# A planned order of 478 jobs replaced by another: gate and output weights at other places among the loads, weight sums among other key jobs

## The chip, the cores and the metric

The kernel runs on one core of a Trainium2 chip. A core has five engines with a queue of instructions each, which work side by side and wait for each other by semaphores: TensorE (PE: matmuls, with their weight loads listed as PEld), VectorE (DVE), ScalarE (ACT), GpSimd (POOL) and SyncE (SP), which here issues nearly all DMA transfers. Matmuls write to PSUM, eight banks; everything else lies in SBUF. The metric is the device time of one launch in microseconds (us), as a median of runs.

## The reference, cut to what matters

One transformer block on x of 2048 rows and 576 columns: modulated layer norm, linear attention over 32 heads of 18 columns with a softmax feature map, a gated residual, a second modulated layer norm, a feed-forward of width 4608 and a second gated residual.

```python
mod = (silu(c) @ w_mod).reshape(1, 6, 1, -1)
sa, ca, ga, sb, cb, gb = ...
h = layernorm(x) * (1 + ca) + sa
q, k, v = h @ wqkv                       # 32 heads of 18
phi_q = concat(softmax(q @ w_phi), softmax(-(q @ w_phi)))
phi_k = concat(softmax(k @ w_phi), softmax(-(k @ w_phi)))
kv, z = phi_k^T v, sum(phi_k)
x = x + ga * ((phi_q @ kv / (phi_q @ z + 1e-6)) @ wo)
h = layernorm(x) * (1 + cb) + sb
x = x + gb * (relu(h @ w1) @ w2)
```

## The kernel before, in words

The 2048 rows are 16 tiles of 128. Keys and values of all 16 tiles have to be summed up (kv) before the first tile can be attended, so the kernel has a long first part that is not a loop: it loads, folds the head matrices into the key and query weights, makes the six modulation rows, projects K, V and Q of all tiles, attends tiles 0 to 3 (4 and 5 begun), and runs the first two-tile block of the feed-forward. Then come seven blocks b = 1 to 7 of two tiles each: the output projection `project` (L967) of the next two tiles, the first layer `l1_seven` (L756), the second layer `l2`. The feed-forward multiplies 2 x 2 blocks of matrices with seven products instead of eight, which is why sums of blocks of the weights w1 and w2 have to be made beforehand on DVE.

The order of the first part is written out as one string, `ORDER`, of 478 words. A word is a job, with a tile or part number, and behind a colon the pair of PSUM banks that its result takes. A loop (L1141) calls the jobs one after the other; each puts its instructions at the end of the queues of its engines, and no scheduler moves them later. So a word's place sets its place in the queue of each engine it uses, and no instruction passes one ahead of it on the same engine.

```python
for word in ORDER.split():
    name, _, s = word.partition(":")
    ...
    if s:
        at[f, n] = pair(int(s))
    JOBS[f](*(() if n is None else (n,)))
```

The jobs that matter below, by engine:

- SP, loads: `Lx` and `Lt` (x by rows and transposed, blocks of tiles), `LwkT`, `LwqT`, `Lwv` (key, query and value weights), `Lwsc`, `Lwsh` (first modulation), `Lwsb`, `Lwcb` (second modulation), `Lwga`, `Lwgb` (gates), `Lwo` (output weight); `wl0` to `wl4` (parts of w1, L612), `w2a0` to `w2a2` and `w2b0`, `w2b1` (parts of w2), `wm0` to `wm7` (further copies of blocks of w1 as operands of the sums, L491; `wm0` and `wm1` take the room of tiles of x that `bn12` to `bn15` have read). `VRd` and `QRd` move the four correction rows of the value and query weights into place; `gaw`/`gar` and `gbw`/`gbr` pass the gate rows through memory; `sq`/`qi` store and load again the query features of tiles 4 to 15; `qt`, `ou`, `hT` are transposes by DMA (L363, L416).
- PE: `Z` (matmuls on zeros that fill idle time, L244), `FK` and `FQ` (folding), `sc`, `sh` (first modulation), `m2` (second modulation, 50 matmuls that read wsb and then wcb, L265), `ga`, `gb` (gate rows, L376), `KR`, `VR`, `QR` (correction rows, also L376), `T` (transposed statistics, L638), `K`, `V`, `Q` (projections of a tile, ten matmuls each, L282; `Ka`, `Kb` are two pieces of the first two), `kv` (L334), `nu` (attention of a tile, L404), `ot` and `ht` (transposes on PE), `W` or `wf`/`wr` (output projection; L957 and L964), `lm0` to `lm8` (first layer of block 0, L739), `pa0` to `pa13` (its second layer, L922).
- DVE: `bn` (statistics of a tile, L249 and L250), `sd` (silu of c), `sK` (sums of a tile's key features, L292), `qs` (the same for queries, L292 and L353), `vE` (scaling a tile of values out of PSUM, L316), `nO` (normalising the attention, L411 and L412), `xr`, `xR` (residual), `lb` (second statistics), `ap`, `hd`, `lu`, `lv`, `px`, `py`, `pf` (block 0), `tf` (sums of features for block 1, L851), `wt0` to `wt7` (sums of blocks of w1, L489), `td`, `tb`, `tc`, `te` (sums of parts of w2, three each, L515).
- ACT: `eK`, `eQ` (exponentials of a tile, L287), `FQra` (folded query weights out of PSUM), `xa` (scaling x by the modulation), `rK`, `sa`, `Tc`, `m2c`, `ha`, `aP`, `hS` and others. POOL: `pA`, `pR`, `pM` (key features), `xp`, `sp`, `qp`, `wo` (output weight times the gate row).

A bank pair is taken again only after the job that empties it: K by `eK`, V by `vE`, Q by `eQ`, FQ by `FQra`, and so on.

Of the kernel before, what the change touches and what calls it, by code (L numbers as in the profile page):

```python
# [42 lines left out]


ORDER = """
Lbdw LwkT Lx0 Lcc sx Lwsc Lwsh Lx2 Lid Lt0 Lwv Lx4 Lt1 Z11 Z1 FK Z2 fra2 frd1 sd rp fra4 LwqT bn1 bn0 frd3 Z3 sc ca
frr bn2 sh shc sa0 sp0 xu0 fra0 T0:0 xv0 Tc0 KR:3 bn3 mk KRh Ka0:1 KRd2 Lx6 sa2 sp2 KRd0 KRd1 VR:0 VRh KRd3 Kb0 eKa0
VRe Ka1:2 VRd bn5 Kb1 eKa1 sK0 Lwsb sK1 Lt2 FQ3:1 FQra3 T2:0 bn7 xp2 Tc2 FQ0:3 FQra0 rK0 K2:2 FQ4:0 K3:1 pR0 FQra4 pA0
bn9 V1:0 FQ2:3 bn6 eK2 pM1 Lwga V0:2 Lwcb eK3 FQra2 vE1 Lx10 V3:1 xp6 sK2 FQ1:3 xa4 FQra1 V2:0 vE0 sK3 rK2 ga:2 gac
gaw pA2 bn4 QR:3 QRh Lt4 vE3 QRe QRd sa4 vE2 m2:2 sp4 bn8 T4:3 Tc4 m2c K4:1 eK4 pM0 kv0 Lt3 wl0 bn10 bn14 pR2 K5:0 eK5  # L50
K6:2 bn11 sa8 kv1 eK6 sK4 pM2 kv2 xp14 K7:0 eK7 Lwgb sK5 Q0:1 pM3 w2b0 bn12 rK4 pA4 V5:2 eQ0 sK7 kv3 vE5 sp8 V4:0 vE4
T8:2 pR4 pM4 xa8 wm0 Tc8 xp10 pM5 Q1:1 K8:0 K9:2 eQ1 eK8 kv4 qs0 qp0 sK6 bn13 gb:1 Q2:0 Lwo eK9 wm3 kv5 rK6 pA6 gbc
Q3:2 V6:1 sK8 eQ2 pR6 eQ3 pM7 sK9 rK8 qs1 qp1 V7:0 pM6 pA8 bn15 sa12 sp12 pR8 pM8 vE7 vE6 V9:2 V8:0 vE9 kv6 K11:1
T12:2 xa12 vE8 wl1 pM9 K10:0 eK11 qs3 wm1 kv7 kv8 qs2 Lmask qp2 sK11 Tc12 qp3 w2a2 K12:1 eK10 sK10 eK12 Q5:2 rK10 pA10
eQ5 sK12 V11:0 vE11 kv9 K13:1 eK13 V10:0 vE10 gar sK13 K14:2 eK14 rK12 wo4 qt0 wt0 pR10 pM10 kv10 K15:0 pM11 kv11 wl3
eK15 pA12 sK14 Q4:2 eQ4 pR12 qt3 pM13 pM12 qt1 sK15 V12:1 sq5 V13:0 vE13 vE12 V14:2 qt2 rK14 pR14 pA14 V15:0 vE14 pM14
pM15 kv12 kv13 sq4 vE15 kv14 kv15 wo0 Q11:1 kz nu1:0 nO1 qi5 eQ11 wo3 nu0:3 Q6:2 ot1:0 nO0 wl2 wo2 Q7:1 oc1 ot0:3 wo1
W1:0 eQ6 qs5 td2 w2b1 sq6 xr1 oc0 Q8:2 W0:0 eQ7 eQ8 sq8 sq11 lb1 lr1 wt1 Q9:1 eQ9 xr0 lb0 lr0 Q12:3 sq7 nu2:2 Q10:0
nu3:1 nO2 ap1 w2a0 sq9 nO3 Q14:2 eQ12 Q13:3 eQ10 ht1:1 eQ14 w2a1 ap0 ht0:0 Q15:2 ou2 ou3 hd td0 tb0 ha eQ13 te0 lm0:1
lu0 lm1:0 te2 tb2 qi4 qs4 sq13 eQ15 sq10 lu1 wl4 wf2:3 wf3:1 wr2 xR2 sq12 gbw xR3 lm2:2 lm5:0 td1 lu2 lb3 qp4 lm6:3  # L60
tb1 wm2 lb2 wm4 lu5 qt4 wt3 lm8:1 wt2 lr3 aP3 tc2 lm3:0 lu6 lr2 aP2 sq14 lm7:2 te1 hT3 gbr lv0 wm7 lu3 wt5 sq15 lu8
lm4:3 wt6 nu4:0 lu4 lu7 lv2 pa0 pa1 lv1 px hT2 qp5 pa2 pa3 tc0 qi6 wt7 py pc0 pa4 pa5 qt5 hS1 pc1 wm6 pa6 pa7 wm5 hS2
qi7 qi8 nO4 ou4 pa8 pc2 wt4 tc1 pf0 nu5:3 nO5 pa9 pf1 pa10 hS0 qs6 tf0 pa11 pa12 pa13 pf2 ou5 qs7 pf3 po1 tf2 qp7 qp6
po0 qt6 qi9 qt7 tf1 tf3
"""
# [1207 lines left out]
```

## Time and profile before

| | us |
|---|---|
| three runs | 373.23, 373.57, 375.97; median 373.57 |
| the profiled execution | 374.58 |
| its span, first to last instruction | 372.8 |
| PE, DVE, ACT, POOL busy in the span | 363.8, 293.0, 233.2, 128.7 |
| granted TensorE clock | 1.00 of full speed |
| DMA, mean over the span | 135 GB/s, 50.28 MB |

The profile is of one execution. A row of its timeline has the start and the length in us, the engine, the line of the kernel, what is written from what, the number of instructions, and in brackets the idle time of the engine before it with what ended it. A row of SPq is an issue: its length is the time at the head of the queue, not that of the transfer. A row of the DMA view ends with the median time from issue to landing. PE's rows overlap, since matmuls are pipelined.

### The profile page before, as it was taken

To read this page: it belongs to the slowest core of one execution; us is meant where nothing else is said; L and a number is where in the kernel's file an instruction comes from. 1 tells how busy PE (TensorE), PEld (TensorE's weight loads), DVE (VectorE), ACT (ScalarE), POOL (GpSimd) and SP (SyncE) were. 2 spreads that over 40 slices of the span, in tenths; PEclk is the share of its full clock that TensorE was granted. 3 is DMA by queue.
4 is the path that set the end of the run, shared out by engine and by line. 5 is a ranking of instruction groups with operands and counts; after the bars stand their busy time and mean duration, and the time that the engine had idled before them with its cause. 6 is when DMAs were issued, how large, how long until landed. Compare 5 with 4: busy or idle time off the path is not lost.

```text
span 372.8 us, 14795 instructions
## 1 busy us (share of the span) xinstructions
PE 363.8 (98%) x6486; PEld 311.9 (84%) x6486; DVE 293.0 (79%) x538; ACT 233.2 (63%) x499; POOL 128.7 (35%) x183
## 2 busy tenths in 40 slices
...
GB/s 291 359 341 203 417 365 296 256 158 343 277 202 238 70 67 98 83 129 85 40 96 128 36 51 115 98 35 70 97 67 19 86 18 51 35 2 36 4 2 33
DMA packets 58913, 50.28 MB, mean 135 GB/s; under 512 B 46944, under 2 KB 51168, under 8 KB 58080
## 3 DMA queue, kind: packets, MB, share of 16 engines
...
q10 hardware_dynamic: 144, 0.16, 0.2%
q14 instruction: 15, 0.12, 0.1%
...
## 4 chain that ended last, share of the span: by engine, by line
PE 88%; DMA 8%; ACT 1%; DVE 1%; SPq 1%; issue 0%; DVEq 0%; ACTq 0%
PE PS L873 29%; PE PS L793 27%; PE PS L282 13%; PE PS L922 4%; PE PS L776 4%; PE PS L739 3%; DMA R<-in_wcb_dram 3%; DMA R<-in_w_dram 2%; PE PS L982 2%; DMA R<-in_xT_dram 2%; PE PS L404 2%; PE PS L334 1%; DMA R<-in_wkT_dram 1%; PE PS L957 1%; PE PS L421 1%; PE PS L910 1%
## 5 line engine op out<-in xcount | busy, mean ns | idle before, releaser
L793 PEld LDWEIGHTS <-R 64*128 64x128 bf16 (+1 forms) x2128 | 88.7, 94 | 0.8 <-issue 0.2
L861 POOL TENSOR_TENSOR yt<-yt,gb_row 128x288 f32<-128x288 f32 x23 | 25.7, 1119 | 180.9 <-DVE yt L860 180.9
L873 PEld LDWEIGHTS <-RH 128*128 128x128 f16 x738 | 71.0, 98 | 18.2
L793 PE MATMUL PS<-h,R 64*128 64x128 bf16 x1232 | 80.9, 216 | 0.0
L823 ACT ACTIVATE RH<-PS 128x512 f16<-128x512 f32 x112 | 59.3, 604 | 10.7 <-PE PS L793 10.5
L873 PE MATMUL PS<-R,RH 128*128 128x288 bf16 (+1 forms) x486 | 65.0, 286 | 0.0
L793 PE MATMUL PS<-RE,R 64*128 64x128 f16 x896 | 56.1, 216 | 0.0
L287 ACT ACTIVATE RT<-PS,rs 128x576 bf16<-128x576 f32 x64 | 43.4, 750 | 11.5 <-PE PS L282 10.5
L793 PE MATMUL PS<-h,early 64*128 64x128 bf16 x448 | 37.3, 216 | 0.0
L1045 ACT ACTIVATE h<-h,mod 128x256 bf16<-128x256 bf16 x63 | 32.8, 588 | 2.1 <-DMA h<-xn 2.1
L873 PE MATMUL PS<-RT,RH 128*128 128x288 f16 x252 | 33.8, 286 | 0.0
L282 PE MATMUL PS<-RH,R 116*128 116x288 bf16 x240 | 32.4, 286 | 0.8 <-DVE RH L522 0.7
L282 PE MATMUL PS<-RH,RT 116*128 116x288 bf16 x240 | 31.9, 286 | 0.0
L793 PEld LDWEIGHTS <-w 64*128 64x128 f16 (+1 forms) x560 | 30.8, 94 | 0.0
L793 PE MATMUL PS<-RE,w 64*128 64x128 f16 x448 | 30.1, 216 | 0.0
L793 PE MATMUL PS<-RE,x_sb 64*128 64x128 f16 x448 | 29.0, 216 | 0.0
L793 PEld LDWEIGHTS <-early 64*128 64x128 bf16 x448 | 28.2, 94 | 0.1
L282 PEld LDWEIGHTS <-R 116*128 116x128 bf16 x240 | 22.5, 98 | 6.6 <-issue 1.0
L282 PEld LDWEIGHTS <-RT 116*128 116x128 bf16 x240 | 22.9, 98 | 5.5
L860 DVE TENSOR_TENSOR yt<-PS,RS 128x288 f32<-128x288 f32 x23 | 10.4, 451 | 20.5 <-PE PS L873 16.6
L249 DVE BATCH_NORM_STATS2 st<-x_sb 128x6 f32<-128x288 bf16 x64 | 25.6, 442 | 0.8 <-DMA x_sb<-in_xk_dram 0.7
L813 ACT ACTIVATE RS<-PS 128x512 f32<-128x512 f32 x14 | 8.4, 597 | 26.9 <-PE PS L793 18.3
...
## 6 DMA issues: line engine op xcount, KB each, us to landing
...
```

The lines of the kernel that those rows point to most:

```text
L249: dve.bn_stats(out=s[:, hf, :], in_=x_sb[:, t % 6 if n else t, hf * HD:(hf + 1) * HD])
L282: pe.matmul(pr[:, k, 0:HD], lhsT=xt(t, ck), rhs=w[0:R, ck, k * HD:(k + 1) * HD], start=(ck == 0), stop=(ck == NC - 1))
L287: act.activation(out=E.rearrange("p (b h s e) -> p b h s e", b=2, s=2, e=DH)[:, :, :, s, :], in_=pr[:, :, 0:HD].rearrange("p b (h e) -> p ...
L739: pe.matmul(pr[:, hf, n * 256 + o:n * 256 + o + w], lhsT=w1_lhs(hf, c, j, h), rhs=hb[b0:b0 + 64, c, o:o + w], start=(n == 0 and c == 0 and ...
L776: pe.matmul(PS[:, bank_at[n], j * 256:j * 256 + 256], lhsT=w1_lhs(hi, c, j, hi), rhs=hb[64 * hi:64 * hi + 64, c, :], start=(j == 0 and c = ...
L793: pe.matmul(PS[:, bank_at[BK[n] + str(g)], i * P:(i + 1) * P], lhsT=w[r, (4 * c + i) * P:(4 * c + i + 1) * P], rhs=x, start=(n in ("M1", " ...
L823: act.activation(out=o, in_=v[{"k11": "Y", "k12": "Z", "k21": "X", "k22": "W"}[n]], func=ACT.Relu)
L860: dve.tensor_tensor(out=y, in0=PS[:, bank, 0:HD], in1=SS[:, s, :], op=ALU.add)
L861: pool.tensor_tensor(out=y, in0=y, in1=gb_row[:, c], op=ALU.mult)
L873: pe.matmul(PS[:, bank, 0:HD], lhsT=am[:, j, :], rhs=bm[:, j, :], start=first and j == 0, stop=(j % 9 == 8), skip_group_check=True)
L922: pe.matmul(PS[:, bank, 0:HD], lhsT=am[:, j, :], rhs=bm[:, j, :], start=(first == 1 and j == 0), stop=(j % 9 == 8), skip_group_check=True)
L1045: act.activation(out=o, in_=o, func=ACT.Identity, scale=mod(1, c), bias=mod(0, c))
```

## The change

`ORDER` is replaced by another string of the same 478 jobs; nothing else is touched. The counts of all instructions stay; the order in all five queues and the bank pairs of some jobs differ. The whole diff:

```diff
@@ -43,25 +43,25 @@
 
 
 ORDER = """
-Lbdw LwkT Lx0 Lcc sx Lwsc Lwsh Lx2 Lid Lt0 Lwv Lx4 Lt1 Z11 Z1 FK Z2 fra2 frd1 sd rp fra4 LwqT bn1 bn0 frd3 Z3 sc ca
-frr bn2 sh shc sa0 sp0 xu0 fra0 T0:0 xv0 Tc0 KR:3 bn3 mk KRh Ka0:1 KRd2 Lx6 sa2 sp2 KRd0 KRd1 VR:0 VRh KRd3 Kb0 eKa0
-VRe Ka1:2 VRd bn5 Kb1 eKa1 sK0 Lwsb sK1 Lt2 FQ3:1 FQra3 T2:0 bn7 xp2 Tc2 FQ0:3 FQra0 rK0 K2:2 FQ4:0 K3:1 pR0 FQra4 pA0
-bn9 V1:0 FQ2:3 bn6 eK2 pM1 Lwga V0:2 Lwcb eK3 FQra2 vE1 Lx10 V3:1 xp6 sK2 FQ1:3 xa4 FQra1 V2:0 vE0 sK3 rK2 ga:2 gac
-gaw pA2 bn4 QR:3 QRh Lt4 vE3 QRe QRd sa4 vE2 m2:2 sp4 bn8 T4:3 Tc4 m2c K4:1 eK4 pM0 kv0 Lt3 wl0 bn10 bn14 pR2 K5:0 eK5
-K6:2 bn11 sa8 kv1 eK6 sK4 pM2 kv2 xp14 K7:0 eK7 Lwgb sK5 Q0:1 pM3 w2b0 bn12 rK4 pA4 V5:2 eQ0 sK7 kv3 vE5 sp8 V4:0 vE4
-T8:2 pR4 pM4 xa8 wm0 Tc8 xp10 pM5 Q1:1 K8:0 K9:2 eQ1 eK8 kv4 qs0 qp0 sK6 bn13 gb:1 Q2:0 Lwo eK9 wm3 kv5 rK6 pA6 gbc
-Q3:2 V6:1 sK8 eQ2 pR6 eQ3 pM7 sK9 rK8 qs1 qp1 V7:0 pM6 pA8 bn15 sa12 sp12 pR8 pM8 vE7 vE6 V9:2 V8:0 vE9 kv6 K11:1
-T12:2 xa12 vE8 wl1 pM9 K10:0 eK11 qs3 wm1 kv7 kv8 qs2 Lmask qp2 sK11 Tc12 qp3 w2a2 K12:1 eK10 sK10 eK12 Q5:2 rK10 pA10
-eQ5 sK12 V11:0 vE11 kv9 K13:1 eK13 V10:0 vE10 gar sK13 K14:2 eK14 rK12 wo4 qt0 wt0 pR10 pM10 kv10 K15:0 pM11 kv11 wl3
-eK15 pA12 sK14 Q4:2 eQ4 pR12 qt3 pM13 pM12 qt1 sK15 V12:1 sq5 V13:0 vE13 vE12 V14:2 qt2 rK14 pR14 pA14 V15:0 vE14 pM14
-pM15 kv12 kv13 sq4 vE15 kv14 kv15 wo0 Q11:1 kz nu1:0 nO1 qi5 eQ11 wo3 nu0:3 Q6:2 ot1:0 nO0 wl2 wo2 Q7:1 oc1 ot0:3 wo1
-W1:0 eQ6 qs5 td2 w2b1 sq6 xr1 oc0 Q8:2 W0:0 eQ7 eQ8 sq8 sq11 lb1 lr1 wt1 Q9:1 eQ9 xr0 lb0 lr0 Q12:3 sq7 nu2:2 Q10:0
-nu3:1 nO2 ap1 w2a0 sq9 nO3 Q14:2 eQ12 Q13:3 eQ10 ht1:1 eQ14 w2a1 ap0 ht0:0 Q15:2 ou2 ou3 hd td0 tb0 ha eQ13 te0 lm0:1
-lu0 lm1:0 te2 tb2 qi4 qs4 sq13 eQ15 sq10 lu1 wl4 wf2:3 wf3:1 wr2 xR2 sq12 gbw xR3 lm2:2 lm5:0 td1 lu2 lb3 qp4 lm6:3
-tb1 wm2 lb2 wm4 lu5 qt4 wt3 lm8:1 wt2 lr3 aP3 tc2 lm3:0 lu6 lr2 aP2 sq14 lm7:2 te1 hT3 gbr lv0 wm7 lu3 wt5 sq15 lu8
-lm4:3 wt6 nu4:0 lu4 lu7 lv2 pa0 pa1 lv1 px hT2 qp5 pa2 pa3 tc0 qi6 wt7 py pc0 pa4 pa5 qt5 hS1 pc1 wm6 pa6 pa7 wm5 hS2
-qi7 qi8 nO4 ou4 pa8 pc2 wt4 tc1 pf0 nu5:3 nO5 pa9 pf1 pa10 hS0 qs6 tf0 pa11 pa12 pa13 pf2 ou5 qs7 pf3 po1 tf2 qp7 qp6
-po0 qt6 qi9 qt7 tf1 tf3
+Lbdw LwkT Lx0 bn1 Z3 Z11 Lcc Lwsc Lwsh Lx2 bn0 sx sd Lid FK frd1 frr mk Lt0 Lwv Lx4 Lt1 LwqT sa0 fra2 Lx6 Z2 frd3 fra4
+sc ca Z1 fra0 bn2 xu0 sh xv0 sp0 T0:1 shc Tc0 bn3 KR:0 KRh KRd1 KRd2 Ka0:3 KRd0 KRd3 VR:1 sa2 Kb0 VRh VRe VRd Ka1:2
+Kb1 sp2 eKa0 bn4 sK0 Lwga T2:3 Lwsb FQ0:1 bn5 FQ3:0 eKa1 sK1 xp2 Tc2 FQra0 K2:2 Lt2 FQra3 rp K3:1 FQ4:3 bn7 eK2 rK0
+FQra4 sK2 pR0 V1:0 pA0 vE1 V0:2 vE0 eK3 FQ1:3 bn6 FQra1 FQ2:1 FQra2 V2:0 QR:3 ga:1 Lwcb sa4 Lx10 pM1 sp4 QRh sK3 Lt4
+QRe V3:2 rK2 bn8 pM0 kv0 gac T4:1 QRd Lwo pA2 vE2 Lt3 gaw Lwgb xp6 xa4 Tc4 kv1 Lmask m2:0 m2c vE3 K5:2 K4:0 eK5 eK4
+bn9 bn11 bn10 pR2 pM2 K6:1 pM3 sK5 sK4 wl4 eK6 gar sa8 kv2 kv3 K7:0 xp14 eK7 Q0:1 sK6 bn12 sp8 rK4 V5:2 wl2 pA4 V4:0
+eQ0 Q1:1 xa8 bn14 pR4 vE5 vE4 T8:2 pM4 kv4 Tc8 K8:0 bn13 eQ1 qs0 K9:2 eK8 gb:1 eK9 bn15 wm1 gbc sK7 pM5 rK6 xp10 kv5
+Q2:0 qp0 wo4 sa12 qs1 qp1 sK9 eQ2 sK8 pA6 Q3:2 wm0 eQ3 V6:1 pR6 pM6 sp12 vE6 V7:0 vE7 rK8 V9:2 pA8 qs3 V8:1 vE8 vE9
+w2b0 K11:0 kv6 wl0 w2a2 T12:1 pM7 xa12 Tc12 qs2 kv7 K10:2 pR8 pM8 eK11 sK11 eK10 kv8 K12:1 Q5:0 eK12 sK10 qp3 qt3 wt0
+qt1 eQ5 K13:2 qp2 rK10 qt2 qt0 V11:1 V10:0 sq5 pM9 kv9 pA10 w2a1 sK12 pR10 eK13 vE11 K14:1 wm3 pM10 vE10 kv10 sK13
+K15:0 pM11 eK14 rK12 qi5 pA12 eK15 pR12 wm2 Q4:2 wt1 pM13 eQ4 V12:1 sK14 sK15 vE12 kv11 V13:0 V14:2 V15:1 pM12 kv12
+vE13 rK14 pR14 pA14 vE14 kv13 pM14 pM15 vE15 kv14 wl1 kv15 Q11:0 eQ11 wo2 kz nu0:2 sq11 nu1:1 Q6:3 eQ6 nO1 Q7:0 sq6
+wo1 ot1:1 oc1 nO0 Q8:2 ot0:3 oc0 qs5 td2 sq4 wo3 wl3 wo0 W1:1 Q9:3 xr1 eQ8 sq8 eQ7 lb1 qi4 td1 eQ9 sq9 w2b1 W0:1 lr1
+xr0 Q12:2 eQ12 Q10:3 eQ10 lb0 ap1 nu2:0 nu3:1 lr0 qp5 sq7 Q14:2 nO3 Q13:3 ht1:1 eQ14 Q15:2 ou3 nO2 ou2 ap0 ht0:0 hd ha
+wt3 sq10 lm0:1 eQ15 qs4 lm1:0 wf3:2 wt2 eQ13 lu0 wf2:3 tb2 wr2 xR3 lu1 xR2 w2a0 gbw wm7 td0 lm2:1 lu2 lb2 lm6:0 lr2
+tb1 gbr te2 lm5:3 lu6 lm7:1 sq14 te1 te0 lb3 aP2 lu5 lu7 lm8:2 wt7 wm5 lr3 aP3 sq13 lv0 tb0 lm3:3 lu3 qt5 tc0 lm4:0
+nu5:3 lu8 wm6 qp4 qt4 sq12 lu4 sq15 lv2 pa0 nO5 hT2 pa1 lv1 pc0 nu4:0 nO4 hT3 qi6 qi8 tc1 tc2 pa2 px ou4 pa4 pa5 pc1
+pa3 wt4 pf0 wm4 pa7 wt5 pa8 pa6 qs6 hS0 ou5 pc2 pa10 py hS1 tf0 pa9 pa11 qi7 pf1 pa12 wt6 pf2 qs7 pa13 pf3 po0 qp6 qt6
+qi9 qp7 qt7 po1 hS2 tf1 tf2 tf3
 """
 
 SEVEN = """
```

On SyncE the loads now stand: ... wqT, x6, VRd, wga, wsb, t2, wcb, x10, t4, QRd, wo, t3, gaw, wgb, mask, m2c, wl4, gar, wl2, wm1, wm0, w2b0, wl0, w2a2, qt3, qt1, qt2, qt0, sq5, w2a1, wm3, qi5, wm2, wl1, sq11, sq6, sq4, wl3, sq8, qi4, sq9, w2b1, sq7, ou3, ou2, sq10, w2a0, gbw and so on. Before they stood: ... wqT, x6, VRd, wsb, t2, wga, wcb, x10, gaw, t4, QRd, m2c, t3, wl0, wgb, w2b0, wm0, wo, wm3, wl1, wm1, mask, w2a2, gar, qt0, wl3, qt3, qt1, sq5, qt2, sq4, qi5, wl2, w2b1, sq6, sq8, sq11, sq7, w2a0, sq9, w2a1, ou2, ou3, qi4, sq13, sq10, wl4, sq12, gbw and so on.

## The prediction

> **What bounds the kernel now.** I read the page first, then the timeline of TensorE (PE) alone, then busy time by stretches, then the queues of the other engines at the places where PE had waited.
>
> ```profile
> span 372.8 us, 14795 instructions
> PE 363.8 (98%) x6486; PEld 311.9 (84%) x6486; DVE 293.0 (79%) x538; ACT 233.2 (63%) x499; POOL 128.7 (35%) x183
> ```
>
> PE works for 363.8 of 372.8 us, and the change keeps every job, so the work stays; only the 9.0 us in which PE stands can grow or shrink. These are the waits in the part that is reordered (brackets: idle time before the row, and what ended it):
>
> ```profile
> 14.95 1.91 PE L282 MATMUL PS<-RH,R 116*128 116x288 bf16 x12 [0.70 <-DVE RH L522]
> 18.10 0.45 PE L273 MATMUL PS<-RS,R 126*128 126x126 bf16 x6 [1.23 <-DMA R<-in_wqT_dram]
> 27.92 0.50 PE L376 MATMUL PS<-R,RS 116*32 116x144 bf16 x20 [0.80 <-DMA R<-in_wga_dram]
> 29.85 0.78 PE L265 MATMUL PS<-siluc,R 116*128 116x1 bf16 x25 [0.28 <-DMA R<-in_wcb_dram]
> 97.55 2.13 PE L957 MATMUL PS<-wo_sb,oT 128*128 128x288 bf16 x16 [1.22 <-DMA oT<-o_sb]
> 102.89 1.21 PEld L739 LDWEIGHTS <-R 64*128 64x128 bf16 x24 [0.41 <-DMA R<-in_w_dram]
> ```
>
> Busy time by stretches (length, then PE, weight loads, VectorE (DVE), ScalarE (ACT), GpSimd (POOL); clock, DMA share, GB/s):
>
> ```profile
> 20.00:30.00 10.00, 8.84 (x141) 7.15 (x139) 8.90 (x19) 8.65 (x22) 5.38 (x11) 1.00 0.95 382
> 30.00:40.00 10.00, 10.00 (x130) 8.39 (x128) 9.07 (x20) 8.65 (x21) 7.25 (x12) 1.00 0.69 232
> 40.00:60.00 20.00, 20.00 (x216) 16.31 (x215) 18.56 (x26) 17.68 (x38) 16.91 (x29) 1.00 1.05 359
> 60.00:90.00 30.00, 30.00 (x328) 24.89 (x327) 24.69 (x37) 20.40 (x38) 16.05 (x24) 1.00 0.80 249
> ```
>
> The six make 0.70 + 1.23 + 0.80 + 0.28 + 1.22 + 0.41 = 4.64 us. From 30 to 90 us PE never stands. What a new order can win is therefore below 4.64 us, 1.2% of the span; what it can lose is open. And another engine is nearly as full near the end of the part:
>
> ```profile
> 90.30:133.10 42.80, 41.41 (x68) 1.00 0.85 202
> ```
>
> DVE is busy for 41.41 of the 42.80 us before the first two-block pass begins. A lead that PE gains counts only as far as DVE gains it too.
>
> **The start, 0 to 18 us: at nothing.** Two statistics jobs (bn1, bn0) go ahead of the silu (sd), and two more idle-filling matmuls ahead of the fold.
>
> ```profile
> 6.92 0.16 DVE L551 TENSOR_SCALAR sg<-sg 116x5 f32<-116x5 f32 x1
> 7.41 0.81 DVE L249 BATCH_NORM_STATS2 st<-x_sb 128x6 f32<-128x288 bf16 x2
> 9.31 0.63 DVE L462 CAST RH<-PS 116x504 bf16<-116x504 f32 x1
> 8.32 0.28 PE L265 MATMUL PS<-siluc,R 116*128 116x1 bf16 x5
> 12.14 0.50 PE L376 MATMUL PS<-RH,RS 116*32 116x144 bf16 x20
> 13.38 0.29 ACT L518 ACTIVATE yt<-PS 128x144 bf16<-128x144 f32 x1
> ```
>
> The two jobs take 9.31 - 7.41 = 1.9 us and the silu 0.5; if they begin at about 6.3, the modulation matmuls begin at about 8.8 instead of 8.32, and with one filler between them the row matmuls (12.14) begin about 0.7 later. What needs them is the copy at 13.38, which stood behind other ACT work for 0.7 us, so that cover takes it up. If the copy slips by a few tenths, the 1.23 us that PE waits for the query weights (18.10) takes that up too: their transfer has the same loads in front as before. Bounds 0 to +0.5; I take 0.
>
> **The gates, 18 to 31 us: -0.6.** The load of the first gate's weights (wga) changes places with wsb and t2: 800 + 640 KB less in front of it.
>
> ```profile
> 19.97 0.97 SPq L217 DMA_DIRECT2D R<-in_wcb_dram  x1
> R<-in_wcb_dram SPq DMA_DIRECT2D x1, 800.0 KB, 9.8
> 30.63 0.25 PE PS L638 x4
> 34.90 0.69 PE PS L334 x18
> ```
>
> 1440 KB, 1.47 MB, at the 382 GB/s of the stretch 20 to 30 is 3.9 us; the gate matmuls come only some 2 us earlier on PE (26.0 for 27.92), so the 0.80 goes. The second modulation (m2) still needs wcb, which has the same four loads in front and lands 9.8 us after its issue at 19.97, near 29.8. PE has T4 (0.25, the chain of waits), kv0 and kv1 (9 of the 18 matmuls of 0.69 each) ahead of it in exchange, 0.9 us, and reaches m2 at about 28.6. It then waits for its bank, which the second value tile (vE2) leaves at about 28.95, and for wcb at 29.8: together about 0.4 where it was 0.28. Sum -0.80 + 0.1, less a little for ACT's new order; bounds -0.9 to 0, I take -0.6.
>
> **31 to 90 us: at nothing.** Here the loads of the second block's weights move, and the weight sums (wt0, wt1) among the key jobs. The danger is SyncE's queue, which is in order:
>
> ```profile
> SPq L493 <- DVE mv L250: 12.2, 2, 10.5
> 40.89 0.76 DVE L316 TENSOR_TENSOR RT<-PS,early 128x576 bf16<-128x576 f32 x1 [0.59 <-PE PS L282]
> 43.21 1.29 DVE L292 TENSOR_REDUCE early<-RT 128x64 f32<-128x1152 bf16 x1
> 45.41 2.61 DVE L292 TENSOR_REDUCE early<-RT 128x64 f32<-128x1152 bf16 x2
> 47.94 1.34 DVE L292 TENSOR_REDUCE Rq<-RT 128x64 f32<-128x1152 bf16 x1
> 49.59 0.76 DVE L249 BATCH_NORM_STATS2 st<-x_sb 128x6 f32<-128x288 bf16 x2
> 65.50 1.22 DVE L489 TENSOR_TENSOR x_sb<-R,x_sb 128x2048 f16<-128x2048 bf16 x1
> ```
>
> SyncE stood 10.5 us until bn15 (49.59) freed the room of wm1. After the change wm1 stands earlier among the loads, and w2b0, wl0 and w2a2 are queued behind it; wl0 had been issued long before. wt0 (65.50) needs wl0, and moves ahead of sK12 to about 59.5. But bn15 moves too: between vE4 (40.89) and it, the sums at 43.21, 45.41 (two) and 47.94 go elsewhere, 1.3 + 2.6 + 1.7 = 5.6 us, so it falls at about 44.2 and SyncE is free at 45. wm1, wm0, w2b0 and wl0 are 3472 KB, 3.56 MB, at 359 GB/s (the stretch 40 to 60) 9.9 us, so wl0 lands near 56: 3 us to spare. On ACT, sa12 goes ahead of eQ2, and PE meets a few banks 0.1 us before they are free. Bounds -0.1 to +2.5 (the second rival); I take 0.
>
> **The attention of tiles 2 and 3, 90 to 104 us: -1.6.**
>
> ```profile
> 86.52 0.47 SPq L606 DMA_DIRECT2D R<-in_w2a_dram  x1
> 90.63 2.56 SPq L416 DMA_TRANSPOSE oT<-o_sb  x2
> oT<-o_sb SPq DMA_TRANSPOSE x2, 6.1
> oT<-o_sb SPq DMA_TRANSPOSE x14, 2.7
> ```
>
> The two transposes before the wait at 97.55 took 6.1 us to land, against a median of 2.7 for all 14: two w2a loads of 864 KB were issued just before them. Now only w2b1 (1296 KB, behind sq9, about 85) and one 288 KB store stand close ahead; 1.62 MB at the 359 GB/s used above are through in 4.5 us, near 90, and w2a0 comes after the transposes. Issued at 90 and 91, they land by 95, and PE wants them at 95.6. The 1.22 goes. Were 6.1 us what such a transpose costs in itself, it would land at 97 and most of the wait would stay: the sum would be about 1 us poorer. [...] The wait of 0.41 at 102.89 goes too: its load (wl4) stands right behind m2c now, and wl3, now the last of its kind, is issued near 79 for a use near 100. PE's own sum is now -0.6 - 1.22 - 0.41 = -2.2.
>
> **What is late next: DVE, 90 to 133 us.**
>
> ```profile
> 98.73 1.35 DVE L292 TENSOR_REDUCE Rq<-RT 128x64 f32<-128x1152 bf16 x1 [0.47 <-DMA RT<-eqd]
> 101.99 1.05 DVE L515 TENSOR_TENSOR RT<-R 128x1728 f16<-128x1728 bf16 x1
> 132.18 0.95 DVE L851 TENSOR_TENSOR RE<-h,RE 128x512 f16<-128x512 bf16 x1
> 133.05 1.41 DVE L429 TENSOR_TENSOR x_sb<-x_sb,PS 128x576 bf16<-128x576 bf16 x2
> 133.97 0.60 PE L776 MATMUL PS<-h,R 64*128 64x256 bf16 x8
> ```
>
> One third of a w2 sum (td1, 101.99) is done before 90 now: -1.0. qi4 is issued behind eQ8, near 82, where it had stood behind the two transposes of 90.63, so the 0.47 before 98.73 goes. Other gaps of one or two tenths come and go: 0 to -0.3. The scaling of tiles 0 and 1 (hd) ends where it did, since its second half follows ht0, which now stands behind Q15. So the last feature sum (132.18) ends about 1.6 us earlier. The residual add behind it (133.05) frees the bank that PE writes at 133.97: its first half ends at about 133.75, 0.2 us of slack. DVE's -1.6 and this slack, against PE's -2.2, give the end: **-1.8**. From there on the code is the same.
>
> Span 372.8 - 1.8 = 371.0. The profiled execution took 374.58, 1.0 above the median of 373.57; from the median the forecast is **371.8 us**.
>
> **Rivals.** 1. *The lead is lost near the end*: the transposes land late again (1.2), or DVE meets new gaps of a microsecond. For it: DVE's 97% and thirty reordered jobs there; against it: the sums above. -1.8 + 1.5: 373.3 us. Chance 0.2.
> 2. *Slower: the first weight sum stops DVE.* If bn15 stays near 50, wl0 lands near 50.4 + 9.9 + 1.5 = 61.8, and DVE stands at wt0 from 59.5 on; the key sums behind it free PE's banks, so PE loses nearly as much, and 2.3 us gives 374.1. It decides from a landing later than 59.5; for 1% more than before (377.3) wl0 has to land 5.5 us after that, or another queue has to stop likewise (the reordered POOL has wo4, which needs the first gate's row, 15 us earlier). Chance 0.15, of it 0.12 over 1%.
> 3. *All waits go and DVE keeps up*: 4.64 less the 1.23 for the query weights, with some tenths from the middle: -3.4 to -4, 369.9 us. Chance 0.04.
>
> **The numbers.** The forecast, -0.8 to -2.8, has 0.61. It, the first rival and the small half of the second lie within 1% (3.7 us, about what a measurement of this kernel can tell from no change): 0.84; faster 0.04, slower 0.12. For 8 in 10 the range runs from 370.4 (the gates' and DVE's best bounds) to 375.2 (the second rival with 3.4 us).
>
> **What would show it.** Right: no wait before the gates' L376 row, none before L957, none for in_w_dram at L739; the L957 row near 96, the first L429 behind the L851 rows near 131.3. Wrong: an idle time before the first L489 on DVE; SyncE's wait at L493 ending near 50; a PE row between 30 and 90 us with a wait above 0.5; L957 waiting for oT again.

## The result and the profile after

The changed kernel takes 373.28 us (median of 20 runs, 372.75 to 375.82); the kernel before, run 20 times, takes 375.38 us (373.23 to 377.59). The ratio is 0.9954 with a 95% interval of 0.9934 to 0.9973, that is 1.0 to 2.5 us less. Two later comparisons gave 0.9946 (0.9921 to 0.997) and 0.9969 (0.9947 to 0.999). The ratios leave out the runs that lie over 1.5% above the fastest of the same kernel (8 of 159 of the kernel before in the comparisons below); the medians do not. The forecast was 371.8 us, 1.8 us under a median of 373.57. The gain at the medians is about the one that was forecast, but the time is 1.5 us above the forecast, and the gain is not made of what the forecast made it of.

The page of the changed kernel, and busy time of PE in the gates' stretch (length, PE; granted clock, DMA share, GB/s):

```profile
span 372.0 us, 14787 instructions
PE 364.3 (98%) x6486; PEld 312.1 (84%) x6486; DVE 292.7 (79%) x538; ACT 232.9 (63%) x499; POOL 131.0 (35%) x183
```

```profile
20.00:30.00 10.00, 9.97 (x169) 1.00 0.98 395
```

The gates' stretch is full now: 9.97 of 10 us where it was 8.84. TensorE's (PE's) timeline after:

```profile
8.73 0.26 PE L265 MATMUL PS<-siluc,R 116*128 116x1 bf16 x5 [0.61 <-DVE siluc L553]
12.92 0.50 PE L376 MATMUL PS<-RH,RS 116*32 116x144 bf16 x20 [0.47 <-DVE RS L682]
18.08 0.72 PE L273 MATMUL PS<-RS,R 126*128 126x126 bf16 x12 [0.59 <-DMA R<-in_wqT_dram]
26.02 0.49 PE L376 MATMUL PS<-R,RS 116*32 116x144 bf16 x20
...
95.52 2.13 PE L957 MATMUL PS<-wo_sb,oT 128*128 128x288 bf16 x16 [0.49 <-DMA oT<-o_sb]
108.18 4.11 PE L739 MATMUL PS<-h,R 64*128 64x256 bf16 x72 [0.35 <-DVE RH L748]
126.72 2.37 PE L922 MATMUL PS<-R,RH 128*128 128x288 bf16 x18 [0.34 <-DVE yt L860]
132.91 0.61 PE L776 MATMUL PS<-h,R 64*128 64x256 bf16 x8 [0.18 <-DVE x_sb L429]
```

The gate row (26.02) has no bracket, 0.80 before. L957 still waits for oT (the attention of tiles 2 and 3, transposed), 0.49 for 1.22, and the load that L739 waited 0.41 for is no longer waited for; there are three small waits for VectorE (DVE) that were not there. VectorE's timeline:

```profile
58.69 1.21 DVE L489 TENSOR_TENSOR x_sb<-R,x_sb 128x2048 f16<-128x2048 bf16 x1
...
100.35 1.06 DVE L515 TENSOR_TENSOR RT<-R 128x1728 f16<-128x1728 bf16 x1 [0.22 <-DMA R<-in_w2a_dram]
114.13 0.56 DVE L752 TENSOR_TENSOR RT<-RH 128x768 f16<-128x768 f16 x1 [0.98 <-DMA eqd<-RT]
130.37 1.83 DVE L851 TENSOR_TENSOR RE<-h,RE 128x512 f16<-128x512 bf16 x2
132.12 1.41 DVE L429 TENSOR_TENSOR x_sb<-x_sb,PS 128x576 bf16<-128x576 bf16 x2
```

The first weight sum (58.69) starts without a wait: the second rival did not come. A wait of 0.98 us for a store is new (eqd is the memory through which the query features pass). The chain of waits (start, length, step) names what stood ahead of oT and of that store:

```profile
89.07 6.41 DMA oT<-o_sb
95.52 2.13 PE PS L957 x16
...
104.28 4.05 SPq L363
...
109.00 5.01 DMA eqd<-RT
```

From this one profile the story seemed plain: PE's lead, 1.1 us at the second gate (L376, 43.93 for 45.03) and 2.0 at L964 (97.59 for 99.61), shrinks to 0.8 at the end, because the transposes and a store land late. The experiments showed that these two waits are draws of the transfers, that is, they come and go between executions of the same kernel, and that something else, which no line of the two profiles shows, goes with about half of the gain.

### The profile page after: what moved, and what is told of

The parts are those of the page before. It is cut to its first block, busy times and chain, and to the rows that moved or that the text cites. A ratio compares the mean times of both kernels' runs of the same rounds, so it can differ in the third digit from the quotient of the medians.

```text
span 372.0 us, 14787 instructions
## 1 busy us (share of the span) xinstructions
PE 364.3 (98%) x6486; PEld 312.1 (84%) x6486; DVE 292.7 (79%) x538; ACT 232.9 (63%) x499; POOL 131.0 (35%) x183
## 4 chain that ended last, share of the span: by engine, by line
PE 83%; DMA 7%; DVE 5%; SPq 2%; issue 1%; ACT 1%; DVEq 0%
PE PS L873 29%; PE PS L793 27%; PE PS L282 15%; PE PS L776 4%; DMA R<-in_wqT_dram 3%; PE PS L982 2%; DMA R<-in_wsc_dram 2%; DMA oT<-o_sb 2%; SPq L363 2%; PE PS L334 2%; PE PS L404 1%; DMA eqd<-RT 1%; PE PS L957 1%; DVE R L489 1%; DVE Rq L292 1%
## 5 line engine op out<-in xcount | busy, mean ns | idle before, releaser
L861 POOL TENSOR_TENSOR yt<-yt,gb_row 128x288 f32<-128x288 f32 x23 | 27.6, 1199 | 185.8 <-DVE yt L860 185.8
L287 ACT ACTIVATE RT<-PS,rs 128x576 bf16<-128x576 f32 x64 | 42.5, 748 | 10.3 <-PE PS L282 9.0
L282 PE MATMUL PS<-RH,R 116*128 116x288 bf16 x240 | 31.5, 286 | 0.3
```

The lines of the kernel that those rows point to most:

```text
L282: pe.matmul(pr[:, k, 0:HD], lhsT=xt(t, ck), rhs=w[0:R, ck, k * HD:(k + 1) * HD], start=(ck == 0), stop=(ck == NC - 1))
L287: act.activation(out=E.rearrange("p (b h s e) -> p b h s e", b=2, s=2, e=DH)[:, :, :, s, :], in_=pr[:, :, 0:HD].rearrange("p b (h e) -> p ...
L861: pool.tensor_tensor(out=y, in0=y, in1=gb_row[:, c], op=ALU.mult)
```

## The experiments

Each comparison below has its own runs of the kernel before, on the same chip. With every run stands the mean clock that TensorE was granted; it takes steps, 1.000, 0.995, 0.991. "At full clock" means a run at 0.998 or more. A "stand" is idle time of an engine.

| run | median us | at full clock | median of these | ratio to before, interval |
|---|---|---|---|---|
| before, with e1 to e4 | 375.29 | 16 of 30 | 374.09 | |
| e1 changed kernel | 373.01 | 11 of 12 | 372.99 | 0.9946 (0.9921 to 0.997) |
| e2 two stores earlier | 372.61 | 7 of 7 | 372.61 | 0.9936 (0.991 to 0.9962) |
| e3 one load earlier | 374.65 | 10 of 12 | 374.58 | 0.9988 (0.9967 to 1.001) |
| e4 both | 375.11 | 12 of 12 | 375.11 | 0.9994 (0.9969 to 1.002) |
| before, with e5 to e8 | 375.17 | 14 of 30 | 374.22 | |
| e5 before | 375.16 | 6 of 12 | 373.85 | 0.9987 (0.995 to 1.0024) |
| e6 gate load alone | 378.42 | 0 of 7 | | 1.0088 (1.0056 to 1.012) |
| e7 weight sum alone | 377.94 | 2 of 12 | 376.34 | 1.0075 (1.0037 to 1.0113) |
| e8 with a key load | 378.41 | 3 of 12 | 375.83 | 1.0078 (1.0045 to 1.0111) |
| before, with e9 to e12 | 375.38 | 18 of 35 | 373.63 | |
| e9 gate stand filled | 374.08 | 10 of 12 | 373.95 | 0.9987 (0.9956 to 1.0019) |
| e10 four stands filled | 374.97 | 12 of 12 | 374.98 | 1.0012 (0.999 to 1.0035) |
| e11 early part alone | 375.72 | 4 of 12 | 374.10 | 1.0027 (0.9992 to 1.0061) |
| e12 late part alone | 375.93 | 5 of 12 | 374.23 | 1.0038 (1.0001 to 1.0076) |
| before, with e13 to e16 | 374.95 | 20 of 35 | 374.21 | |
| e13 changed kernel | 373.48 | 12 of 12 | 373.48 | 0.9969 (0.9947 to 0.999) |
| e14 gate step undone | 374.60 | 10 of 12 | 374.38 | 0.9989 (0.9958 to 1.0019) |
| e15 oT step undone | 374.28 | 9 of 12 | 374.21 | 0.9992 (0.9962 to 1.0023) |
| e16 key load behind its sum | 374.27 | 10 of 10 | 374.27 | 0.9978 (0.9956 to 1.0001) |
| before, with e17, e18 | 374.70 | 10 of 17 | 373.69 | |
| e17 key load late | 380.47 | 0 of 4 | | 1.0140 (1.0089 to 1.0191) |
| e18 as e2 | 373.03 | 12 of 13 | 373.01 | 0.9951 (0.9923 to 0.998) |

### e1: the changed kernel again

> The changed kernel once more, on the same chip as the three that follow, as their yardstick. If the profile of the changed kernel is typical, TensorE again waits about 0.5 us for oT ahead of L957, VectorE about 1.0 us for a store of eqd ahead of an L752 near 113 us, and the time stands about 2 us below the kernel before. If that profile was one draw of transfers that land now here, now there, the 0.5 and the 1.0 change by half or more while the time stays within 0.3 us.

The two waits were a draw: neither comes in the profiles of e1, e2 and e13. In the profile of e1 no L957 waits (the row at 94.90 has no bracket), VectorE does not wait for the store, and the span is 371.1 us. The load of the second block's weights ahead of the transposes landed 8.4 us after its issue where the first profile had 10.0:

```profile
R<-in_w2b_dram SPq DMA_DIRECT2D x2, 1296.0 KB, 8.4
```

The chain of waits of e1 shows what the prediction had called the end of this part:

```profile
107.40 0.36 DVE RH L748
107.81 4.11 PE PS L739 x72
...
114.98 13.23 PE PS L922 x108
```

VectorE's list is on the chain up to 107.40, TensorE's own behind it, and the last feature sums end 2.0 us earlier than in the kernel before (VectorE's timeline; 132.18 + 0.95 there):

```profile
129.26 1.82 DVE L851 TENSOR_TENSOR RE<-h,RE 128x512 f16<-128x512 bf16 x2
```

When no store is late, VectorE sets the time up to 107.40 us and not up to the first L429, as the prediction had it.

### e2 and e18: two stores ahead of the slow transpose

```diff
-... lm7:1 sq14 te1 te0 ...
-... qp4 qt4 sq12 lu4 sq15 lv2 ...
+... lm7:1 sq14 sq12 sq15 te1 te0 ...
+... qp4 qt4 lu4 lv2 ...
```

> The changed kernel with two stores of column planes (the ones issued behind the transpose whose issue took 4.05 us, the second of them at 109.00 us) issued ahead of it, directly behind the store before. Theory A, that VectorE's list sets the end of this stretch (it runs without a gap over 0.15 us from that store's landing to the first L429): its 0.98 us wait at L752 goes, TensorE's 0.34 at L922 and 0.18 at the first two-tile L776 go with it, and the kernel becomes 0.5 to 0.9 us faster than the changed one. Theory B, that TensorE's own list and the oT wait set it: the 0.98 goes and the time stays within 0.2 us. Theory C, that the stores only change places with transposes that are as urgent: the transposes land later by a store's 2 us and a new wait near 110 us takes the gain back or more.

> The changed kernel with the two stores ahead of the transpose once more, since the two looks at the changed kernel before it differed: in one, VectorE waited 0.98 us for such a store, in three others not at all or 1.57 (where another load was moved). If the stores' place removes the late draws, no run at full clock is above 373.6 us (of 43 of the changed kernel 12 are), and the median stays at 372.6. If the first seven runs were a lucky draw, it comes out at 373.0 to 373.5, as the changed kernel.

0.4 us under the changed kernel in the one comparison (372.61 for 373.01), but e1 beside it had no 0.98 to remove. Over both comparisons the 19 runs at full clock have a median of 372.98 and none above 373.6 us; of 43 such runs of the changed kernel (median 373.27) 15 are above (the expectation says 12, a miscount). So the move seems to cut late draws, and gives at most 0.3 to 0.4 us (the two sets of runs are from different chips); theory A's 0.5 to 0.9 had mistaken a draw for the rule.

### e3 and e4: the load ahead of oT one place earlier

```diff
-... sq4 wo3 wl3 wo0 ... eQ9 sq9 w2b1 W0:1 lr1
+... sq4 wo3 w2b1 wl3 wo0 ... eQ9 sq9 W0:1 lr1
```

> The changed kernel with the load of 1,296 KB for the second block (issued at 84.09 us, landed at 94.12, directly ahead of oT's transposes, landed 95.22 and 95.80) issued one load earlier, ahead of the key load of 78.39 us. If the transposes were late because that load stood ahead of them, they land about 6.4 - 4 = 2 to 3 us after their issue, near 92, and the 0.49 us wait of L957 goes. What it does to the end then tells the bound: by theory A (VectorE sets the end up to 131 us) the kernel gains 0 to 0.2 us, by theory B (TensorE and oT set it) the whole 0.5. If the transposes are late for another reason (6.4 us is what they take behind any load), the wait stays.

> The changed kernel with both moves, of the two stores and of the load. Theory A: at most 0.2 us over what the stores give alone, so 0.5 to 1.0 us faster than the changed kernel. Theory B: 0.5 us, all of it from the load. If each move clears one of two bounds that lie side by side, neither alone gives more than 0.3 us and both together give 0.8 to 1.2.

No wait for oT is left, but e3 is 1.6 us slower than e1, and e4 2.1: none of the theories. Two loads now stand ahead of three stores. ScalarE (ACT) and TensorE in e3:

```profile
89.24 1.38 ACT L287 ACTIVATE RT<-PS,rs 128x576 bf16<-128x576 f32 x2 [1.68 <-DMA eqd<-RT]
```

```profile
90.67 1.39 PE L282 MATMUL PS<-RH,RT 116*128 116x288 bf16 x10 [1.27 <-ACT RT L287]
```

ScalarE waits for a store to free its buffer, and TensorE for ScalarE. The store was issued at 81.60, behind the load that was moved, and landed 7.56 us later (chain of waits of e3); in e1, where that load is issued behind this store, the same ScalarE row comes at 87.46 for 89.24 and waits for no store. So the load that was moved ahead delayed the stores behind it.

### e5: the kernel before again

> The kernel before once more, on the same chip as the three that follow. Its times so far lie between 373.2 and 377.6 us, those of the changed kernel mostly between 372.7 and 374.1. If the spread comes from transfers that land now in time, now late, its profile differs from the first one in the waits for DMA between 60 and 105 us (1.22 us for oT at L957 and 0.41 for a key load at L739 in the first), by a microsecond or more in sum; if it comes from the chip, the waits are the same to 0.2 us and the clock or the ends of the span differ.

It was both. The stand for oT was 0.49 here (1.22 in the first profile), and the rows at the gate are followed by something new. PE's timeline, then its busy time by microsecond:

```profile
27.88 0.50 PE L376 MATMUL PS<-R,RS 116*32 116x144 bf16 x20 [0.74 <-DMA R<-in_wga_dram]
28.85 0.76 PE L265 MATMUL PS<-siluc,RE 116*128 116x1 bf16 x25 [0.15 <-ACT gt L380]
29.82 0.81 PE L265 MATMUL PS<-siluc,R 116*128 116x1 bf16 x25 [0.20 <-DMA R<-in_wcb_dram]
```

```profile
29.00:30.00 1.00, 0.80 (x32) 1.00 0.94 393
30.00:31.00 1.00, 1.00 (x29) 0.51 0.76 179
...
33.00:34.00 1.00, 1.00 (x14) 0.79 0.23 89
```

The column behind the count is the granted clock. Behind 0.74 + 0.15 + 0.20 us of standing, TensorE ran at half clock (0.50) for 3.4 us, 30.0 to 33.4. PE is "busy" all the while, so no wait shows it, but 1.7 us of work are lost: 0.0046 of the span, the step of 0.995. Over all 159 runs of the kernel before that have a clock beside them, 84 are at full clock (median 373.97 us), 46 one step down (375.95), 28 two (377.77), 1 three; the median of all is 375.11. The spread of the kernel before is, for the most part, a count of such stretches; runs with the same count still lie up to 3 us apart. Of 44 runs of the changed kernel, 43 are at full clock.

### e6 to e8: one step of the change alone

```diff
-... Kb1 eKa1 sK0 Lwsb sK1 Lt2 ... pM1 Lwga V0:2 ...
+... Kb1 eKa1 sK0 Lwga Lwsb sK1 Lt2 ... pM1 V0:2 ...
```

> The kernel before with one step of the change alone: the first gate's weights are issued ahead of the second stem weights. My prediction put this part at -0.6 us at 30 us (the 0.80 us wait of the first L376 for its weights goes, some 0.2 of other waits come up). If the lead is kept to the end, the kernel is 0.6 us faster than before; if the wait for oT, which is set by transfers, is where TensorE and the transfers meet, the lead is eaten there (that wait grows from 1.22 by the lead) and the time stays within 0.2 us.

```diff
-... eQ14 w2a1 ap0 ht0:0 Q15:2 ou2 ou3 hd ...
+... eQ14 ap0 ht0:0 Q15:2 ou2 ou3 w2a1 hd ...
```

> The kernel before with another step alone: the load that stood ahead of oT's transposes (issued 86.52, landed 96.89 us) goes behind them. If oT was late because of it, TensorE's 1.22 us wait at L957 goes; the load for the last key job of the first set, which landed at 102.84 and was waited for 0.41 us, is then met earlier by that much and waited for about 1.5, so the end gains 0.2 us at most. If oT's lateness does not come from the load ahead of it, the 1.22 stays to within 0.3.

```diff
-... kv11 wl3 eK15 ... lu1 wl4 wf2:3 ...
+... kv11 wl3 wl4 eK15 ... lu1 wf2:3 ...
```

> As the run before it, and with the last key load issued early too, directly behind the key load before it. Both waits of TensorE in this stretch then go (1.22 for oT, 0.41 for the key load). My prediction put both together at -2.2 us on TensorE at 104 us, cut by VectorE's list to -1.6 to -1.8 at the end: so 1.3 to 1.6 us faster than before if that holds. If VectorE's list or a store keeps TensorE up behind 104 us as in the changed kernel, 0.6 to 1.0. If loads moved ahead hold up the stores behind them, no gain.

All three are 2.8 to 3.3 us slower than before, outside every expectation. In e6 the load of t2, a block of x transposed, comes one place later, ScalarE's in-order list stands 2.86 us for it, and the matmuls beside the gate wait for a copy further down that list. In e7, the load that went behind oT's transposes is now issued directly ahead of a read-back (93.95 for 94.63), where it had 6.8 us between (86.52 for 93.28), and VectorE stands for that read-back. ScalarE of e6, PE of e6, VectorE of e7 and PE of e7:

```profile
27.29 2.10 ACT L570 ACTIVATE R<-R,ca 116x256 bf16<-116x256 bf16 x5 [2.86 <-DMA R<-in_xT_dram]
```

```profile
29.97 0.50 PE L376 MATMUL PS<-RH,RS 116*32 116x144 bf16 x20 [2.44 <-ACT RH L576]
```

```profile
101.55 1.35 DVE L292 TENSOR_REDUCE Rq<-RT 128x64 f32<-128x1152 bf16 x1 [3.19 <-DMA RT<-eqd]
```

```profile
103.62 13.63 PE L739 MATMUL PS<-h,R 64*128 64x256 bf16 x216 [2.98 <-DVE RH L748]
```

In e7 the wait for oT did go, as the prediction had it, and the wait for the key load too; 3 us came up elsewhere. e8's PE stands 2.83 us at the same place. In e6's profile the clock is halved from 31.4 to 34.9 us, in e7's and e8's behind these stands (103.9 to 107.3 and 104.2 to 107.6). Of 31 runs of the three, 5 are at full clock.

### e9 and e10: the stands filled, not shortened

```diff
+    def fill(n, o, z):
+        for _ in range(n):
+            pe.matmul(o[:, 0, 0:512], lhsT=z[:, 0:P], rhs=z[:, 0:512], start=True, stop=True)
...
+        "Y": lambda i: fill(i, at["Y", i], zero if i != 4 else flat(wo_sb)),
...
-... sK3 rK2 ga:2 gac
+... sK3 rK2 Y3:2 ga:2 gac
```

e10 has also Y2:3 ahead of Kb0, Y5:1 ahead of FQ3:1 and Y4:3 ahead of wf2:3.

> The kernel before, with three matmuls on zeros put in front of the first gate's twenty (L376), where TensorE stands 0.74 to 0.80 us for the gate's weights; their result is overwritten. No wait is shortened. In the profile of the kernel before as run again, TensorE's granted clock is 0.50 from 30.0 to 33.4 us, directly behind that stand and two of 0.15 and 0.20 us, and over 72 runs of it the mean clock takes steps: 36 runs at 1.00 (median 374.15 us), 24 at 0.995 (375.97), 12 at 0.991 (378.06). Theory C, that the stand itself makes the clock halve for 3.4 us and that this is half of what the change gained: runs at full clock stay at 374.2 within 0.3, the share of the others falls from 36 of 72 to under a quarter, and the median falls by 0.8 to 1.2 us. If the halving hangs on the whole first 30 us or on the chip, the shares stay as they are and the time with them.

> As the run before, with matmuls whose result is overwritten in front of all four longest stands of the kernel before: two near 14.3 us (0.70), five near 16.9 us (1.23), three at the gate (0.80), four ahead of oT's L957 (1.22). No wait is shortened. Theory C: every run is at full clock, 374.2 us within 0.3, and what is left to the changed kernel (373.0 to 373.3) is what its shorter waits give, 0.9 to 1.2 us. If fillers cost (weights and banks in the way of the work behind them), the runs at full clock are slower than 374.2 by up to the 3.0 us that the fourteen fillers take.

This is the test of the clock. With the gate's stand filled, 10 of 12 runs are at full clock where the kernel before beside it had 18 of 35, and the median falls by 1.3 us though nothing is earlier: the runs at full clock are not faster (373.95 for 373.63). With all four filled, 12 of 12. That is 2 halved runs of 24 for 17 of 35: theory C holds in that filled stands bring the clock back. e9's twelve runs alone could be luck, and the interval of its ratio, 0.9956 to 1.0019, does not exclude no change. e10 is 1.35 us slower at full clock, and its profile does not show by what: its gate row stands 0.3 us later than in the first profile of before (28.19 for 27.92) and the first matmuls on oT 0.1 (97.64 for 97.55). PE in e9, with no bracket at the gate:

```profile
27.63 0.81 PE L248 MATMUL PS<-early 128*128 128x512 bf16 x2
28.38 0.50 PE L380 MATMUL PS<-R,RS 116*32 116x144 bf16 x20
```

(The five lines added above it move the gate from L376 to L380, and the first row holds two of the three fillers; the record of the third is missing.)

### e11 and e12: one half of the change

e11 has the changed order up to kv1 (31 us), then the remaining jobs in the order of before; e12 the order of before up to kv0, then the remaining jobs in the changed order. The seams:

```diff
-... Tc4 kv1 Lmask m2:0 m2c vE3 K5:2 ...
+... Tc4 kv1 bn9 vE3 m2:2 m2c K4:1 eK4 wl0 ...
```

```diff
-... K4:1 eK4 pM0 kv0 Lt3 wl0 bn10 bn14 ...
+... K4:1 eK4 pM0 kv0 Lwo Lt3 Lwgb kv1 Lmask K5:2 ...
```

> The changed kernel's order up to the value sums behind the gates (31 us), and for all jobs behind them the order of before. My prediction gave this part -0.6 us at 31 us. If the lead is kept and the stand at the gate was the source of the halved clock, it is 0.6 us faster at full clock and the share of halved runs falls below a quarter: 1.4 to 1.8 us under the median of before. If the transfers hold oT where it was, L957's wait grows by the lead, from 1.22 (0.49 in the run of before with a halved clock at 30 us) to about 1.9, the time at full clock stays as before, and that longer stand halves the clock there instead.

> The other half: the order of before up to 31 us, and the changed kernel's for all jobs behind. My prediction gave this part -1.2 at the end. If the parts add up, it is 0.4 to 1.2 us faster than before at full clock, and the share of runs with a halved clock stays near half of all, since the stand at the gate is there. If the loads of the changed kernel need the early part's place in SyncE's queue, a wait for a load of the second block's weights (L489, L739) comes up and it is slower than before.

At full clock neither is faster than before (374.10 and 374.23 for 373.63), and the clock is halved as often or more often. In e11 the seam puts a statistics job and a value copy ahead of m2, and PE stands for them; in e12 the stand at the gate is there:

```profile
30.40 0.76 PE L265 MATMUL PS<-siluc,RE 116*128 116x1 bf16 x25 [1.56 <-DVE RT L316]
```

```profile
28.16 0.50 PE L376 MATMUL PS<-R,RS 116*32 116x144 bf16 x20 [1.19 <-DMA R<-in_wga_dram]
...
147.51 0.21 PE L793 MATMUL PS<-RE,x_sb 64*128 64x128 f16 x1 [0.80 <-issue]
```

e12's last row is a gap for which the profile shows no cause, in code that is the same in all kernels; with another of 0.33 at 142.96 it takes 1.1 us of that profile. The halves bring waits of their own at the seam, so they don't weigh the parts; that is what e14 and e15 are for.

### e13 to e15: one step taken back

> The changed kernel again, as the yardstick on the chip of the three that follow. By what the runs showed so far: 11 of 12 runs or more at full clock, 373.0 to 373.3 us, TensorE's lead over the kernel before's first profile 0.8 to 2.1 us at 148 us, according to how late the load ahead of oT's transposes lands.

```diff
-... sK0 Lwga T2:3 Lwsb ... K2:2 Lt2 FQra3 ...
+... sK0 T2:3 Lwsb ... K2:2 Lt2 Lwga FQra3 ...
```

> The changed kernel with one step taken back: the first gate's weights are issued behind the second stem weights and the third block of x, as before. The gate stays early in TensorE's order, so the load is waited for longer than the 0.80 us of before: near 26.0 to 28, about 2 us. Theory C (a stand within the clock's stretch of 3.4 us halves it): nearly all runs have at least one halved stretch (as 10 of 12 and 7 of 7 runs did behind stands of 2.4 to 3.0 us), 1.7 us each, and the lead of 1.1 us at 47 us is gone: 2.5 to 3.5 us slower than the changed kernel. If TensorE has slack behind the gate, the 2 us come back before 47 us, and only the clock's 1.7 stay.

```diff
-... nO3 Q13:3 ht1:1 eQ14 Q15:2 ou3 ... xR2 w2a0 gbw ...
+... nO3 Q13:3 ht1:1 eQ14 Q15:2 w2a0 ou3 ... xR2 gbw ...
```

> The changed kernel with the other step taken back: one load of 864 KB for a weight sum is issued ahead of oT's two transposes again, where the kernel before had one. In five profiles with the order of before, the first transpose landed 0.61 to 0.68 us behind that load, which itself took 8.8 to 10.6 us. If a transpose lands only when the loads issued ahead of it have, oT lands about 2 us later (near 96.5 to 97), L957 waits 1.5 to 2.5 us, and the kernel is 1 to 2 us slower, more where the clock halves. If the step was worth little because VectorE's list sets the end, under 0.5 us.

PE in e14, PE in e15, and e15's busy time by microsecond behind it:

```profile
27.43 0.50 PE L376 MATMUL PS<-R,RS 116*32 116x144 bf16 x20 [1.05 <-DMA R<-in_wga_dram]
```

```profile
97.35 3.44 PE L957 MATMUL PS<-wo_sb,oT 128*128 128x288 bf16 x16 [2.11 <-DMA oT<-o_sb]
```

```profile
97.00:98.00 1.00, 0.65 (x6) 0.99 1.18 382
98.00:99.00 1.00, 1.00 (x7) 0.50 0.46 134
...
101.00:102.00 1.00, 1.00 (x18) 0.80 1.15 206
```

Each step taken back costs the kernel 0.7 to 0.9 us at full clock (374.38 and 374.21 for 373.48) and 0.8 to 1.1 at the median, less than was expected (2.5 to 3.5 and 1 to 2). These sizes are rough, since the runs at full clock overlap: 372.85 to 375.01 in e13, 373.68 to 376.17 in e14, 373.04 to 375.11 in e15. Each cost is about the whole gain at full clock on this chip (374.21 to 373.48), so the two don't seem to add. e15's profile shows why for its step: the lead won at the gate is waited away at L957 (97.35, where the kernel before had 97.55). For e14, whose profile ends at 372.0 for 372.8 of the first of before, no profile shows it. e15 may overstate its step, since the load stands behind a larger one there than in the kernel before. e14's stand was 1.05 us, not 2, and was followed by a halved clock in 2 of 12 runs; e15's, as expected, 2.11, with 3 of 12. So putting the gate's load back brought back few halved runs (2 of 12, where the kernel before had 15 of 35 on this chip): the full clock of the changed kernel may not hang on that load alone.

### e16 and e17: the second rival made on purpose

```diff
-... w2b0 K11:0 kv6 wl0 w2a2 ... qp3 qt3 wt0 qt1 ... qt2 qt0 V11:1 ...
+... w2b0 K11:0 kv6 w2a2 ... qp3 qt3 wt0 qt1 ... qt2 qt0 wl0 V11:1 ...
```

> The second rival of the prediction, made on purpose: the changed kernel with the key load for the first weight sum (issued 45.79, landed 56.62, needed at 58.69) issued behind the four transposes near 61 us. It then lands near 66. By the rival, VectorE stops at that sum from 58.7 to about 66, the key sums behind it hold TensorE's banks, and TensorE loses nearly as much: 5 to 7 us slower than the changed kernel, and a halved clock stretch on top. If TensorE has enough banks and other work, it loses less than half of VectorE's stop.

In e16 the sum wt0 stands ahead of its load and so does not wait: it adds what its buffer held before. The run tells nothing of the rival. But it is one more draw of the same schedule: VectorE waited 1.57 us for the store that cost 0.98 in the first profile and nothing in e1 and e13.

```profile
114.62 0.56 DVE L752 TENSOR_TENSOR RT<-RH 128x768 f16<-128x768 f16 x1 [1.57 <-DMA eqd<-RT]
```

```diff
-... w2b0 K11:0 kv6 wl0 w2a2 ... qp3 qt3 wt0 qt1 ...
+... w2b0 K11:0 kv6 w2a2 ... qp3 qt3 wl0 wt0 qt1 ...
```

> The second rival of the prediction, made on purpose: the changed kernel with the key load for the first weight sum (issued 45.79, landed 56.62, the sum at 58.69) issued behind the first of the four transposes, directly ahead of that sum, near 57.2 us. With nothing else under way it lands 4 to 5.5 us later, at 61 to 63, so VectorE stops at L489 for 2.5 to 4 us. By the rival the key sums behind it hold TensorE's banks and TensorE loses nearly as much: 2 to 3.5 us slower than the changed kernel, and a halved stretch of the clock in a part of the runs. If TensorE has work in hand (VectorE had seven waits of 0.3 to 1.1 us for TensorE between 56 and 81 us, 4.4 us in sum), it loses under 1 us.

VectorE and PE of e17, then PE's busy time by stretches:

```profile
64.34 1.23 DVE L489 TENSOR_TENSOR x_sb<-R,x_sb 128x2048 f16<-128x2048 bf16 x1 [5.18 <-DMA R<-in_w_dram]
```

```profile
67.55 2.56 PE L282 MATMUL PS<-RH,RT 116*128 116x288 bf16 x10 [4.72 <-DVE RT L316]
```

```profile
66.00:67.00 1.00, 0.00 (x0) 0.83 1.14 272
67.00:73.00 6.00, 5.45 (x30) 0.50 0.95 304
73.00:74.00 1.00, 1.00 (x8) 0.75 1.06 427
```

The load landed 6.78 us after its issue at 57.54, where 4 to 5.5 had been estimated. The rival's mechanism is right: of VectorE's 5.18 us TensorE loses 4.72. But the clock is then halved (0.50) from 66.7 to 73.5 us, two stretches, and the kernel is about 7 us slower than the changed kernel (380.47, four runs), half as much again as the stop. The prediction's price for this rival, 2.3 us for a landing 2.3 us late, had no clock in it.

## Where the prediction was right, and where it was wrong

- **The start, at nothing: right.** The modulation and row matmuls come 0.4 and 0.8 us later, and the wait for the query weights falls from 1.23 to 0.59 (it is 0.42 to 1.21 in the later profiles of this start).
- **The gates, -0.6: right in kind, a little too small.** The 0.80 went, and the gate row came at 26.02 (26.0 forecast). m2 waits 0 to 0.22 in three profiles of the changed kernel, and PE leads the first profile of before by 0.8 to 1.2 us in them at the second gate (45.03 before; 43.93, 43.86 and 44.22). e14 puts the step at 0.9 us at full clock, roughly.
- **31 to 90 us, at nothing: right, and for the reason given.** PE is full (no row waits between 18.08 and 95.52), SyncE's load for the freed room goes out at 43.91 (45 forecast), and the first weight sum does not wait: its load landed 1.8 us ahead of it (56.88 for 58.69). e17 shows what a landing too late would have cost: 7 us.
- **oT and the key load, -1.6: right in mechanism; the size was that of one draw.** The key load's 0.41 went. The transposes do land behind the load issued ahead of them: the first transpose lands 0.6 us after that load in the first profile of before (97.50 for 96.89) and 1.1 us after it in that of after (95.48 for 94.38), and e15, which puts a load back, brings the stand back (2.11). But the load took 8.4, 9.1 and 10.0 us in three profiles of the changed kernel, where the prediction had 4.5. So the stand was 1.22 and 0.49 us in two profiles of before, and 0.49, 0 and 0 in three of after.
- **VectorE next, -1.8 at the end: right in the order of things, and again one draw.** The last feature sums (L851) end 0.9, 2.0 and 1.7 us earlier than in the first profile of before (first profile of after, e1, e13; -1.6 forecast), and the span is 0.8, 1.7 and 1.4 us shorter. The new gap of a microsecond, the first rival's, came in the first profile (0.98) and not in e1 or e13.

Three steps failed. The first is "**from the median the forecast is 371.8 us**". The 1.8 us were worked out on the profiled execution of 374.58 us, which had the 1.22 us stand, and then taken off a median of three runs, 373.57. The execution itself gives 374.58 - 1.8 = 372.8, and the changed kernel's profiled runs took 373.77, 372.85 and 373.13. The median of three was a lucky one: that of 159 runs is 375.11, and even that of the 84 at full clock 373.97. The first rival's 373.3 us, which is what was measured, starts from the same 373.57, so that its number came true is luck: its late store and transposes came in one profile of three.

The second is the term of the transposes, "**1.62 MB at the 359 GB/s used above are through in 4.5 us**". The 359 GB/s are of 40 to 60 us; the prediction's own row of 60 to 90 us has 249. The load took 8.4 to 10.0 us, the first transpose landed at 95.48 in the first profile and not by 95, and 0.49 of the 1.22 us stayed there. With that and the late store the span fell by 0.8 us; in e1 and e13, without the two, by 1.7 and 1.4.

The third is "**what a new order can win is therefore below 4.64 us**". The bound was not passed, but it counts a stand at its own length, and half clock behind a stand stands in no such sum: stands at the gate of 1.1 us in all cost 1.7 us more in e5, and about half of all runs of the kernel before have a halved stretch. At the median of the comparison of e1, the gain from 375.29 to 373.01 is 2.28 us; at full clock, 374.09 to 372.99, it is 1.10; the remaining 1.2 go with the clock. With e13 it is 1.47, of it 0.73 at full clock and 0.7 with the clock. So the path gained 0.7 to 1.1 us, not 1.8 (the profile on which the 1.8 was worked out, 374.58, lies 0.6 above the median of its kernel at full clock), and the clock made up for the rest. The profile of before on which the prediction stood had full clock throughout, so it could not show this; the three times, from 373.23 to 375.97, could have raised the question.

That filled stands restore the clock is shown by e9 and e10 together. That it is the gate's stand alone is not: only e9 fills it alone, and e14, with 1.05 us there, mostly kept full clock. Why two stretches come in 28 of 159 runs, and at which stands, is open too.
